# One kernel of attention and an MLP: shared q buffers with batch 3's q loaded first, block 3's sums in one round, and merged bursts of scores

## The chip, the cores and the metric

One core of a Trainium2 chip. The metric is the device time of one execution in microseconds (us). The TensorE is busy almost throughout, and an effect of 1 us is 0.2%; between executions the old kernel itself scatters by 0.8 us in the first rounds and by 1.8 to 3.3 us in later ones.

## The reference, cut to what matters

```python
# q, k, v: (8 batches, 8 heads, 1024, 64); E, F: (64, 1024)
k_proj = einsum('ks,bhsd->bhkd', E, k);  v_proj = einsum('ks,bhsd->bhkd', F, v)
attn   = softmax(q @ k_proj^T / 8)                 # 64 columns for each row
x      = (attn @ v_proj) as (8192 tokens, 512)
h      = x @ w_in                                  # 512 -> 2048
out    = (h * sigmoid(1.702 h)) @ w_out            # 2048 -> 512
```

## The kernel before

The 8192 tokens are 16 blocks of 512, two to a batch. A block runs 16 groups of four 128x512 matmuls with w_in (slots 0 to 15), then eight parts of eight with w_out (slots O to O+7, where O = 16). Attention of later blocks is put between these: `at(block, slot, ...)` says where. GpSimd (POOL) issues the loads of k, q and v, which also cast them to bf16; SyncE (SP) issues everything else in its own order: transposes of q and of the projected k, the stores of the output, and the trip of the softmax's reciprocals.

```python
def load(b):                                # on POOL's queue
    load_kv(k, kt, b, "k_sb")
    if b == 1: load_kv(v, vt, b, "v_sb")
    load_q(b)                               # eight pieces
    if b > 1:  load_kv(v, vt, b, "v_sb")    # v is last
...
def proj(b):                                # projection of k and v: 8 x (k, v)
    for j in range(J):
        for e, r in enumerate((LO, HI)):
            nc.tensor.matmul(kvps[b][r], eft(...), (kt, vt)[e][b][:, :, j, :], ...)
...
def sums(h):                                # one group: softmax sums of a whole block
    ...  nc.tensor.matmul(d_ps[e][32*p:32*p+32], ones[r, :32], expT[h][r, p, :], ...)
    ...  nc.vector.reciprocal(rden[:, e, :], d_ps[e])
def spread(h):                              # "the trip": to DRAM, back as a broadcast
    nc.sync.dma_start(out=rdr, in_=rdens.pop(h)[0:P:32])                   # 16 KB
    for e, r in enumerate((LO, HI)):                                       # 2 x 512 KB
        nc.sync.dma_start(out=rbc[h][r], in_=rdr[None, :, e, :].to_broadcast([D, HP, TB]))
def norm(h, u):                             # sums spread by the matmul itself: no trip
    eight(d_ps, [ones, ones], e);  eight(n_ps, [vqs..., ], e)
    for i in range(2):
        nc.vector.reciprocal(rd, d_ps[i])
        nc.vector.tensor_tensor(x_of(h)[:, 2*u+i, :], n_ps[i], rd, op=ALU.mult)
def values(h, u):                           # uses rbc, what the trip brings
    eight(n_ps, [vqs..., ], ...)
    ...  nc.vector.tensor_tensor(x_of(h)[...], n_ps[i], rbc[h][...], op=ALU.mult)
...
at(2, 0, proj(2), kv_out(2))
at(2, 1, norm(3, 0))
at(2, 11, norm(3, 1))
at(2, O, q_dma(3))
at(2, O + 4, scores(5, 0))
at(2, O + 6, proj(3), kv_out(3), scores(5, 1), sums(4), spread(4))
```

The softmax here doesn't subtract the row's maximum and nothing guards it: scores larger than these inputs give would overflow.

Of the kernel before, what the change touches and what calls it, by code (L numbers as in the profile page):

```python
# [9 lines left out]
F32 = mybir.dt.float32  # L10
BF16 = mybir.dt.bfloat16
# [6 lines left out]
def kernel(ctx, tc, q, k, v, E, F,  # L18
                                                     moe_w_in, moe_w_out, out):
    nc = tc.nc  # L20
    B, H, S, D = q.shape
    KP, _ = E.shape
    DM, DFF = moe_w_in.shape
    P = 128
    J = S // P
# [4 lines left out]
    TB = 512  # L30
    JB = TB // P
# [5 lines left out]
    ldpool = ctx.enter_context(tc.tile_pool(name="ldpool", bufs=1))  # L37
# [3 lines left out]
    ps_x = ctx.enter_context(tc.tile_pool(name="ps_x", bufs=4, space=PSUM))  # L41
# [8 lines left out]
    kt, vt, qt = {}, {}, {}  # L50

    def load_kv(src, dst, b, name, hs=H, js=0, jn=J):
        if b not in dst:
            dst[b] = ldpool.tile([P, H, J, D], BF16, name=name)
        sv = src[b].rearrange("h (p j) d -> p h j d", p=P)
        for h, n in [(h, hs) for h in range(0, H, hs)] if isinstance(hs, int) else hs:
            nc.gpsimd.dma_start(out=dst[b][:, h:h + n, js:js + jn], in_=sv[:, h:h + n, js:js + jn])  # L57

    def load_q(b):
        qt[b] = ldpool.tile([P, J, H, D], BF16, name="q_sb")  # L60
        qv = q[b].rearrange("h (p j) d -> p j h d", p=P)
        for j in range(J):
            nc.gpsimd.dma_start(out=qt[b][:, j], in_=qv[:, j])  # L63

    def load(b):
        load_kv(k, kt, b, "k_sb")
        if b == 1:
            load_kv(v, vt, b, "v_sb")
        load_q(b)
        if b > 1:  # L70
            load_kv(v, vt, b, "v_sb")

# [3 lines left out]
    def load_w_in(i):  # L76
        sl = slice(i * DFF // 8, (i + 1) * DFF // 8)
        nc.gpsimd.dma_start(out=w_in_sb[:, :, sl], in_=w_in_v[:, :, sl])
# [4 lines left out]
    load_kv(k, kt, 0, "k_sb", ((0, 4), (4, 2), (6, 2)))  # L83
    ident = consts.tile([P, P], BF16)
    make_identity(nc, ident)
    load_kv(q, qt, 0, "q0_sb", H, 0, 2)
    load_kv(v, vt, 0, "v_sb", ((0, 4), (4, 2), (6, 2)))
    load_kv(q, qt, 0, "q0_sb", H, 2, 2)
    for i in range(6):
        load_w_in(i)  # L90
    load_kv(q, qt, 0, "q0_sb", H, JB, JB)
    for i in range(6, 8):
        load_w_in(i)
    for i in range(4):
# [34 lines left out]
    def f_tile(shape, dt=F32):  # L129
        return ps_f.tile(shape, dt, name="f_ps")  # L130
# [23 lines left out]
    def eft(j, cols=slice(0, 2 * KP)):  # L154
        return efts[j // (J // 2)][:, j % (J // 2), cols]
# [4 lines left out]
    def proj(b):  # L160
        def go():
            kvps[b] = f_tile([P, H, D])
            for j in range(J):
                for e, r in enumerate((LO, HI)):
                    nc.tensor.matmul(kvps[b][r], eft(j, slice(e * KP, (e + 1) * KP)),  # L165
                                     (kt, vt)[e][b][:, :, j, :],
                                     start=(j == 0), stop=(j == J - 1))
        return go
# [38 lines left out]
    def v_out(b, v_ps):  # L207
        vv = v_ps[HI].rearrange("k (u x) d -> k u x d", x=4)
        for r, xs_ in ((LO, X_LO), (HI, X_HI)):
            if b == 1:  # L210
                vx = vx1[r, :, :D].rearrange("k (u x) d -> k u x d", x=4)
                nc.vector.tensor_copy(vx[:, :, xs_], vv[:, :, xs_])
            nc.vector.tensor_copy(vqs[b % 2][r].rearrange("k (u e) d -> k u e d", e=2), vv[:, :, xs_, :])

    def kv_out(b):
        def go():
            ps = kvps.pop(b)
            k_b = att.tile([KP, H, D], BF16, name="k_b")
            nc.vector.tensor_copy(k_b, ps[LO])  # L219
            if b > 1:  # L220
                nc.sync.dma_start_transpose(out=kts[b % 2], in_=k_b.rearrange("k h d -> k (h d)"))
            v_out(b, ps)
            kbs[b] = k_b
        return go
# [31 lines left out]
    def eight(outs, lhsTs, rhss):  # L256


        for i, ro in ((0, (LO, HI)), (1, (HI, LO))):
            for c in range(0, KP, 32):  # L260
                for ri, r in zip((LO, HI), ro):
                    nc.tensor.matmul(outs[i][r.start + c:r.start + c + 32], lhsTs[i][ri, c:c + 32], rhss[i][ri],  # L262
                                     start=True, stop=True)

    def scores(h, u, half=None):
        b, c = divmod(h, NB2)
        j0, n = (c * JB, JB) if half is None else (c * JB + half * JB // 2, JB // 2)
        ts = slice(j0 * P - c * TB, (j0 + n) * P - c * TB)

        def go():  # L270
            if h not in expT:
                expT[h] = att.tile([P, HP, TB], BF16, name="expT", bufs=3)
            s_ps = [f_tile([P, n * P]) for _ in range(2)]
            eight(s_ps, [kts[b % 2][:, 2 * u + i, :] for i in range(2)],
                 [q0s[half][u][:, :, i, :] if h == 0 else qT[b][:, j0:j0 + n, 2 * u + i, :]
                   for i in range(2)])
            for i in range(2):
                nc.scalar.activation(expT[h][:, 2 * u + i, ts], s_ps[i], AF.Exp, scale=scale)  # L278
        return go
# [4 lines left out]
    def x_of(h):  # L284
        if h not in xT:
            xT[h] = att.tile([P, KC, TB], BF16, name="xT", bufs=3)
        return xT[h]

    def sums(h):


        def go():
            d_ps = [ps_x.tile([P, TB], F32, name="x_ps") for _ in range(2)]
            for p in range(HP):
                for e in range(2):
                    r = HI if (p + e) % 2 else LO
                    nc.tensor.matmul(d_ps[e][32 * p:32 * p + 32], ones[r, :32], expT[h][r, p, :], start=True, stop=True)  # L297
            rden = att.tile([P, 2, TB], F32, name="rden", bufs=1)
            for e in range(2):
                nc.vector.reciprocal(rden[:, e, :], d_ps[e])  # L300
            rdens[h] = rden
        return go

    def spread(h):
        def go():
            rdr = dram.tile([HP, 2, TB], F32, name="rdr")
            nc.sync.dma_start(out=rdr, in_=rdens.pop(h)[0:P:32])
            rbc[h] = att.tile([P, HP, TB], F32, name="rbc")
            for e, r in enumerate((LO, HI)):
                nc.sync.dma_start(out=rbc[h][r], in_=rdr[None, :, e, :].to_broadcast([D, HP, TB]))  # L310
        return go

    def norm(h, u):
        def go():
            e = [expT[h][:, 2 * u + i, :] for i in range(2)]
            d_ps = [ps_x.tile([P, TB], F32, name="x_ps") for _ in range(2)]
            eight(d_ps, [ones, ones], e)
            n_ps = [ps_x.tile([P, TB], F32, name="x_ps") for _ in range(2)]
            eight(n_ps, [vqs[h // NB2 % 2][:, 2 * u + i, :] for i in range(2)], e)
            for i in range(2):  # L320
                rd = att.tile([P, TB], F32, name="rdn")
                nc.vector.reciprocal(rd, d_ps[i])  # L322
                nc.vector.tensor_tensor(x_of(h)[:, 2 * u + i, :], n_ps[i], rd, op=ALU.mult)
        return go

    def values(h, u):
        def go():
            n_ps = [ps_x.tile([P, TB], F32, name="x_ps") for _ in range(2)]
            eight(n_ps, [vqs[h // NB2 % 2][:, 2 * u + i, :] for i in range(2)],
                  [expT[h][:, 2 * u + i, :] for i in range(2)])  # L330
            for i in range(2):
                nc.vector.tensor_tensor(x_of(h)[:, 2 * u + i, :], n_ps[i], rbc[h][:, 2 * u + i, :], op=ALU.mult)  # L332
        return go
# [82 lines left out]
    def at(j, slot, *fs):  # L416
        fill.setdefault((j, slot), []).extend(fs)

    O = FC
    Q = 2 * FC  # L420
# [25 lines left out]
    q_tr0(1, 1, DV)  # L446

    order = [(half, fc) for fcs in (range(12), range(12, FC)) for half in range(2) for fc in fcs]
    at(0, 0, scores(0, 0, 1))
    at(0, 1, scores(0, 1, 1), gelu_table)  # L450
    for p in range(HP):
        at(0, 2 + p, tok(0, p, 1))
        at(0, 5 + p, x_tr(0, p, 1))
    at(0, 20, q_tr(2))
    at(0, 23, q_tr(3))
    for u in range(2):
        at(0, Q + u, scores(1, u))
    at(0, Q + 1, gelu_table)
    for p in range(HP):
        at(0, Q + (2, 4, 6, 7)[p], tok(1, p, 0), tok(1, p, 1))  # L460
# [3 lines left out]
    at(1, 13, lambda: k_tr(1, kbs[1], 0))  # L464
    at(1, 1, q_dma(1, 0, JB), q_dma(1, JB, JB))
    for u in range(2):
        at(1, O + u, scores(2, u))
        at(1, O + 3 + u, scores(3, u))
        at(2, O + 2 * u, scores(4, u))
    for p in range(HP):  # L470
        at(1, O + 2 + p, tok(2, p, 0), tok(2, p, 1))
        at(1, O + 3 + p, x_tr(2, p, 0), x_tr(2, p, 1))
    at(1, O + 5, gelu_table)
    at(1, O + 4, q_dma(2))
    at(2, 0, proj(2), kv_out(2))
    at(2, 1, norm(3, 0))
    at(2, 11, norm(3, 1))
    at(2, O, q_dma(3))
    at(2, O + 4, scores(5, 0))
    at(2, O + 6, proj(3), kv_out(3), scores(5, 1), sums(4), spread(4))  # L480
    at(2, O + 7, gelu_table)
    for b in range(4, B):
        j = NB2 * b - 4
# [65 lines left out]
```

## Time and profile before

| | |
|---|---|
| time, median of 4 | 512.28 us (511.82 to 512.57) |
| TensorE busy | 504.4 of 510.4 us |
| its listed waits after 21 us | one, of 0.2 us |
| POOL's loads, share of the DMA engines | 51.4% over the span |

TensorE sets the time. The prediction below shows the lines that say so. A line of a timeline has start, length (both in us), engine, source line, operation, output<-inputs, tile form, size and count, and in brackets the idle time before it and what ended it (PE is the TensorE, DVE VectorE, ACT ScalarE, SPq the queue of SyncE). f_ps and x_ps are tiles in PSUM, gT and xT what the large matmuls read, k_sb, q_sb and v_sb the loads, rden, rdr and rbc the reciprocals on their trip. One more view matters for what came: the stretches in us from the start, with the busy time and the number of instructions of each engine, the granted TensorE clock, the mean share of the DMA engines (more than 1 when packets overlap) and GB/s.

```profile
117.00:119.00 2.00, 2.00 (x11) 0.78 (x8) 0.00 (x0) 0.59 (x1) 0.00 (x0) 1.00 1.30 295
119.00:121.00 2.00, 2.00 (x25) 0.86 (x29) 0.00 (x0) 0.00 (x0) 0.00 (x0) 1.00 1.23 74
121.00:123.00 2.00, 2.00 (x25) 0.80 (x24) 1.83 (x4) 1.09 (x2) 1.38 (x2) 1.00 0.00 0
```

The DMA engines are loaded without a break until about 120 us and idle only at 121. The projection of batch 3, which needs v(3), the last load in the queue, begins at 119.11. v(3) was issued at 105.97 and landed 10.6 us later, so it had 2.5 us of room. (The time from issue to landing, here and below, is from the DMA view of a window about the issue.) I did not look at this before I predicted.

### The profile page before, as it was taken

What the parts mean: (1) busy time and instruction counts of PE and PEld (TensorE: products, weight loads), DVE (VectorE), ACT (ScalarE), POOL (GpSimd) and SP (SyncE); (2) the same over time, 40 slices, a digit from 0 to 9 for tenths busy, and PEclk for the clock granted to TensorE, in tenths of its full rate; (3) what the DMA queues carried; (4) which work ended last, traced back from release to release, by engine and by line L of the source; (5) the groups of instructions that cost most, each with busy time, mean ns of one, the idle gap of its engine ahead of it and who ended that gap; (6) DMA issues with size and microseconds to landing.
All of it is one profiled execution on the core that took longest, in us unless ns stands there. A gap on an engine that the chain in (4) does not pass through costs nothing.

```text
span 510.4 us, 7234 instructions
## 1 busy us (share of the span) xinstructions
PE 504.4 (99%) x3090; PEld 232.0 (45%) x3090; DVE 165.6 (32%) x221; ACT 264.3 (52%) x443; POOL 78.1 (15%) x97
## 2 busy tenths in 40 slices
PE   8999999999999999999999999999999999999997
PEld 4684444444444444444444444444444444444444
DVE  5513114765161623216161341616214161611000
ACT  2675564555637456471746637374563737244351
POOL 7442051514200051000510033000000000000000
PEclk9999999999999999999999999999999999999999
DMA  9999999999999099651998249990603205050202
GB/s 172 197 203 207 212 140 165 225 177 138 166 239 211 1 209 187 144 129 39 213 167 202 49 99 212 116 241 1 171 1 74 93 9 157 1 166 1 82 1 82
DMA packets 124752, 67.64 MB, mean 133 GB/s; under 512 B 92288, under 2 KB 116096, under 8 KB 122800
## 3 DMA queue, kind: packets, MB, share of 16 engines
q0 software_dynamic: 84400, 29.37, 51.4%
q1 hardware_dynamic: 40240, 37.56, 29.3%
q8 instruction: 24, 0.39, 0.3%
q10 hardware_dynamic: 80, 0.26, 0.2%
q14 instruction: 8, 0.07, 0.0%
HBM read 71.83 MB, written 16.97 MB: 174 GB/s over the span
## 4 chain that ended last, share of the span: by engine, by line
PE 94%; DMA 4%; POOL 1%; issue 0%; DVE 0%; ACT 0%; POOLq 0%
PE f_ps L405 43%; PE f_ps L373 43%; PE f_ps L165 3%; DMA w_in_sb<-in_moe_w_in_dram 2%; PE f_ps L262 2%; DMA v_sb<-in_v_dram 2%; PE x_ps L262 1%; PE x_ps L297 1%; POOL k_sb L57 0%; PE x_ps L359 0%; PE x_ps L344 0%; PE f_ps L397 0%; PE f_ps L244 0%; POOL q_sb L57 0%; POOL v_sb L57 0%
## 5 line engine op out<-in xcount | busy, mean ns | idle before, releaser
L405 PE MATMUL f_ps<-w_out_sb,gT 128*128 128x512 bf16 x1008 | 227.2, 379 | 0.0
L373 PE MATMUL f_ps<-xT,w_in_sb 128*128 128x512 bf16 (+1 forms) x1088 | 226.4, 367 | 0.3 <-DMA w_in_sb<-in_moe_w_in_dram 0.2
L376 ACT ACTIVATE gT<-f_ps 128x512 bf16<-128x512 f32 (+1 forms) x270 | 151.8, 574 | 61.4 <-PE f_ps L373 60.2
L373 PEld LDWEIGHTS <-w_in_sb 128*128 128x128 bf16 x1088 | 105.3, 98 | 116.2 <-issue 1.7
L405 PEld LDWEIGHTS <-gT 128*128 128x128 bf16 x1008 | 95.6, 98 | 120.5 <-issue 11.3
L408 ACT COPY o_sb<-f_ps 128x512 f32<-128x512 f32 x63 | 37.0, 587 | 126.8 <-PE f_ps L405 117.0
L332 DVE TENSOR_TENSOR xT<-x_ps,rbc 128x512 bf16<-128x512 f32 x48 | 30.9, 686 | 201.3 <-PE x_ps L262 124.9
L300 DVE RECIPROCAL rden<-x_ps 128x512 f32<-128x512 f32 x24 | 78.7, 3322 | 10.3 <-PE x_ps L297 10.3
L63 POOL DMA_DIRECT2D q_sb<-in_q_dram x56 | 49.1, 901 | 52.0 <-DMA k_sb<-in_k_dram 39.2
L278 ACT ACTIVATE expT<-f_ps 128x512 bf16<-128x512 f32 (+1 forms) x68 | 35.1, 571 | 32.7 <-PE f_ps L262 32.6
L57 POOL DMA_DIRECT2D k_sb<-in_k_dram x10 | 8.4, 846 | 175.5 <-PE f_ps L165 159.1
L219 DVE CAST k_b<-f_ps 64x512 bf16<-64x512 f32 x7 | 4.8, 683 | 46.8 <-PE f_ps L165 46.8
L278 ACT ACT_TABLE_LOAD x13 | 16.7, 1283 | 4.7 <-PE f_ps L262 4.5
L282 ACT ACT_TABLE_LOAD x14 | 18.0, 1283 | 0.2
L322 DVE RECIPROCAL rdn<-x_ps 128x512 f32<-128x512 f32 x4 | 13.4, 3353 | 0.8 <-PE x_ps L262 0.8
L165 PE MATMUL f_ps<-k_sb,eft 128*64 128x512 bf16 x56 | 13.4, 382 | 0.0
L165 PE MATMUL f_ps<-v_sb,eft 128*64 128x512 bf16 x56 | 13.4, 381 | 0.0
L399 DVE COPY o_sb<-f_ps 128x256 f32<-128x256 f32 x1 | 0.4, 424 | 38.6 <-issue 38.6
L135 PE MATMUL x_ps<-zeros 128*128 128x512 bf16 x34 | 11.2, 450 | 1.2 <-DVE zeros L106 1.2
L262 PE MATMUL f_ps<-qT,kt 64*32 64x512 bf16 x240 | 12.3, 386 | 0.0
L262 PE MATMUL x_ps<-expT,vq 64*32 64x512 bf16 x208 | 10.2, 377 | 0.0
L262 PEld LDWEIGHTS <-kt 64*32 64x32 bf16 x272 | 3.9, 88 | 13.7 <-issue 13.5
(71 smaller groups left out, 128.4 us busy)
## 6 DMA issues: line engine op xcount, KB each, us to landing
out_dram<-o_sb SPq DMA_DIRECT2D x15, 1024.0 KB
rbc<-rdr SPq DMA_DIRECT2D x24, 512.0 KB
k_sb<-in_k_dram POOLq DMA_DIRECT2D x7, 1024.0 KB, 13.3
v_sb<-in_v_dram POOLq DMA_DIRECT2D x7, 1024.0 KB, 10.6
q_sb<-in_q_dram POOLq DMA_DIRECT2D x56, 128.0 KB, 12.0
w_in_sb<-in_moe_w_in_dram POOLq DMA_DIRECT2D x8, 256.0 KB, 12.2
w_out_sb<-in_moe_w_out_dram POOLq DMA_DIRECT2D x4, 512.0 KB, 14.7
out_dram<-o_sb SPq DMA_DIRECT2D x3, 256.0 KB
```

The lines of the kernel that those rows point to most:

```text
L63: nc.gpsimd.dma_start(out=qt[b][:, j], in_=qv[:, j])
L165: nc.tensor.matmul(kvps[b][r], eft(j, slice(e * KP, (e + 1) * KP)), (kt, vt)[e][b][:, :, j, :], start=(j == 0), stop=(j == J - 1))
L262: nc.tensor.matmul(outs[i][r.start + c:r.start + c + 32], lhsTs[i][ri, c:c + 32], rhss[i][ri], start=True, stop=True)
L278: nc.scalar.activation(expT[h][:, 2 * u + i, ts], s_ps[i], AF.Exp, scale=scale)
L282: nc.scalar.preload_act_table(AF.Gelu_apprx_sigmoid)
L300: nc.vector.reciprocal(rden[:, e, :], d_ps[e])
L322: nc.vector.reciprocal(rd, d_ps[i])
L332: nc.vector.tensor_tensor(x_of(h)[:, 2 * u + i, :], n_ps[i], rbc[h][:, 2 * u + i, :], op=ALU.mult)
L373: nc.tensor.matmul(h_ps, w_in_sb[:, kc, fc * P:(fc + 1) * P], xT[j][:, kc, ts], start=(kc == 0), stop=(kc == KC - 1))
L376: nc.scalar.activation(gts[j][:, fc, ts], h_ps, AF.Gelu_apprx_sigmoid)
L405: nc.tensor.matmul(o_ps[n], gts[j][:, fc, n * P:(n + 1) * P], w_out_sb[:, fc, :], start=(fc == 0), stop=(fc == FC - 1))
L408: nc.scalar.copy(osb[j][:, n, :], o_ps.pop(n))
```

## The change

Intent: fewer switches between the large matmuls and the small 64x32 tiles, one group of small matmuls fewer, and a load order that clears the way for the new trip of block 3. Its core (cut and condensed):

```diff
+    def q_buf(order):                      # two q buffers for all batches
+        return ldpool.tile([P, J * H * D], BF16, name="q_sb", bufs=2).rearrange(...)
     def load(b):
+        if b == 3:
+            load_q(b)
         load_kv(k, kt, b, "k_sb")
...
-        load_q(b)
+        if b != 3:
+            load_q(b)
...
-            s_ps = [f_tile([P, n * P]) for _ in range(2)]
+            s_ps = [(x_tile() if x else f_tile([P, TB]))[:, :n * P] for _ in range(2)]
...
-    at(0, 0, scores(0, 0, 1))
-    at(0, 1, scores(0, 1, 1), gelu_table)
+    at(0, 1, scores(0, 0, 1), scores(0, 1, 1, True), gelu_table)
-        at(0, Q + u, scores(1, u))
+        at(0, Q, scores(1, u, None, u > 0))
-        at(1, O + u, scores(2, u))
-        at(1, O + 3 + u, scores(3, u))     # now both at O + 6
-        at(2, O + 2 * u, scores(4, u))
+        at(1, O, scores(2, u, None, u > 0))
+        at(2, O, scores(4, u, None, u > 0))
+        at(2, O + 3 * u, values(3, u))
...
-    at(2, 0, proj(2), kv_out(2))
-    at(2, 1, norm(3, 0))
-    at(2, 11, norm(3, 1))
+    at(2, 0, proj(2), kv_out(2), sums(3), spread(3))
-    at(2, O + 4, scores(5, 0))
+    at(2, O + 3, scores(5, 0))
```

More of the change, by code (lines that the diff above doesn't have):

```diff
@@ L57, in load_kv @@
             nc.gpsimd.dma_start(out=dst[b][:, h:h + n, js:js + jn], in_=sv[:, h:h + n, js:js + jn])
+    def q_buf(order):
+        return ldpool.tile([P, J * H * D], BF16, name="q_sb", bufs=2).rearrange(
+            f"p ({order} d) -> p {order} d", d=D, h=H)
     def load_q(b):
-        qt[b] = ldpool.tile([P, J, H, D], BF16, name="q_sb")
+        qt[b] = q_buf("j h")
         qv = q[b].rearrange("h (p j) d -> p j h d", p=P)
@@ L85 @@
     make_identity(nc, ident)
-    load_kv(q, qt, 0, "q0_sb", H, 0, 2)
+    qt[0] = q_buf("h j")
+    load_kv(q, qt, 0, "", H, 0, 2)
     load_kv(v, vt, 0, "v_sb", ((0, 4), (4, 2), (6, 2)))
-    load_kv(q, qt, 0, "q0_sb", H, 2, 2)
+    load_kv(q, qt, 0, "", H, 2, 2)
     for i in range(6):
         load_w_in(i)
-    load_kv(q, qt, 0, "q0_sb", H, JB, JB)
+    load_kv(q, qt, 0, "", H, JB, JB)
     for i in range(6, 8):
@@ L263, in eight, with x_tile, scores @@
                                      start=True, stop=True)
-    def scores(h, u, half=None):
+    def x_tile():
+        return ps_x.tile([P, TB], F32, name="x_ps")
+    def scores(h, u, half=None, x=False):
         b, c = divmod(h, NB2)
@@ L472 @@
         at(1, O + 3 + p, x_tr(2, p, 0), x_tr(2, p, 1))
-    at(1, O + 5, gelu_table)
+    for u in range(2):
+        at(1, O + 6, scores(3, u, None, u > 0))
+    at(1, O + 6, gelu_table)
     at(1, O + 4, q_dma(2))
-    at(2, 0, proj(2), kv_out(2))
-    at(2, 1, norm(3, 0))
-    at(2, 11, norm(3, 1))
+    at(2, 0, proj(2), kv_out(2), sums(3), spread(3))
     at(2, O, q_dma(3))
-    at(2, O + 4, scores(5, 0))
+    at(2, O + 3, scores(5, 0))
     at(2, O + 6, proj(3), kv_out(3), scores(5, 1), sums(4), spread(4))
```

## The prediction

> **What bounds the kernel now.** I read the engine shares first, then the chain of work that ended last, then the waits of the TensorE, then the timelines of blocks 0 to 3. A "block" is 512 tokens: 64 matmuls with w_in, then 64 with w_out. The attention of later blocks is put between them.
>
> ```profile
> PE 504.4 (99%) x3090; PEld 232.0 (45%) x3090; DVE 165.6 (32%) x221; ACT 264.3 (52%) x443; POOL 78.1 (15%) x97
> ...
> PE 94%; DMA 4%; POOL 1%; issue 0%; DVE 0%; ACT 0%; POOLq 0%
> ...
> PE f_ps L373 <- DMA w_in_sb<-in_moe_w_in_dram: 0.2, 1, 0.2
> ...
> 27.51 4.98 PE L373 MATMUL f_ps<-xT,w_in_sb 128*128 128x256 bf16 x44 [0.20 <-DMA w_in_sb<-in_moe_w_in_dram]
> ```
>
> TensorE is the bound and hardly waits: after 21 us the only listed wait is 0.2 us for a piece of w_in, at 27.51. So DVE or POOL time is worth nothing in itself, and the change gains only what it takes off the TensorE's own row. What a small burst costs there stands in the PE timeline of block 2 and of its neighbours:
>
> ```profile
> 105.59 1.89 PE L405 MATMUL f_ps<-w_out_sb,gT 128*128 128x512 bf16 x8
> 107.41 0.41 PE L262 MATMUL f_ps<-qT,kt 64*32 64x512 bf16 x8
> 107.75 3.63 PE L405 MATMUL f_ps<-w_out_sb,gT 128*128 128x512 bf16 x16
> ...
> 137.07 1.89 PE L405 MATMUL f_ps<-w_out_sb,gT 128*128 128x512 bf16 x8
> 138.89 0.41 PE L262 MATMUL f_ps<-qT,kt 64*32 64x512 bf16 x8
> 139.11 0.40 PE L297 MATMUL x_ps<-expT,ones 64*32 64x512 bf16 x8
> 139.33 0.40 PE L262 MATMUL x_ps<-expT,vq 64*32 64x512 bf16 x8
> 139.66 10.53 PE L405 MATMUL f_ps<-w_out_sb,gT 128*128 128x512 bf16 x48
> ```
>
> Read the start column. A stream of 128x512 matmuls goes at 0.216 us each (16 from 107.75 to 111.31, less the switch). Eight take 1.73, so of the 2.16 us from 105.59 to 107.75 the burst takes 0.43. The burst of three groups at 138.89 takes 139.66-137.07-1.73 = 0.86. Hence a group of eight 64*32 matmuls costs 0.215 us and the two changes of tile form round a burst cost 0.215 us together, however many groups it holds. These two numbers size the gain.
>
> **What the Trainium skill says.** "TensorEngine Tiling (Array Packing)", section Key Properties: changing the tiling mode drains the TensorE. The trace agrees: 0.215 us per burst. "DMA: Bandwidth & Descriptors", section Queues, rings and completion order: each DMA engine goes round the queues packet by packet, so a transfer on one queue is slowed by what another queue has pending; the trace agrees (the reciprocals' trip through DRAM, below). "ScalarE: Activation LUTs", section What ACT_TABLE_LOAD costs: about 1283 ns; the trace has 1283 ns for each of 27 loads. The change keeps their number, so I give that no time.
>
> **The change, part by part.**
>
> *Scores in one burst.* Merged are the two half-width bursts of block 0's second half, and the pairs for blocks 1, 2, 3 and 4: five bursts fewer. The first lies before 27.51, where the TensorE waits for w_in whose transfer the change does not touch: its 0.2 to 0.35 us become a longer wait, worth 0. Blocks 1, 2, 3: 3 x 0.215 = 0.65 us, all ahead of the projection of batch 2. Block 4's: 0.215.
>
> *Block 3's sums in one round.* Each old norm was one burst of two groups, at slots 1 and 11 of block 2. That makes four groups; the new form has one group of sums and two of values: one group less, 0.215. Bursts in block 2 before: slots 1, 11, O, O+2, O+4 (and O+6, kept), where O is the first slot of the w_out half. After: the sums directly behind the projection, O with three groups (scores and values), O+3 with two. Behind a projection a group costs less than alone: the projection with two groups takes 121.52-119.11 = 2.41 us against 1.85 for one alone (64.56 to 66.41), so two groups cost 0.56, and of that 0.43 is the groups. From five separate bursts to two and a cheap one: 2.4 x 0.215 = 0.51, block 4's merge included. Block 2 in all: 0.51 + 0.215 = 0.73 us.
>
> *DVE.* It loses four reciprocals of 3.353 us and adds two of 3.322, minus 6.8 us, off the path. Added are three small DMAs and 1 MB of broadcast for block 3.
>
> *Two q buffers, q(3) first.* The old POOL waits for a free q buffer sum to 1.1 us (on the qT transposes, at 93.62), so a second buffer alone buys nothing. Its worth is the order: load(3) can send q(3) right behind v(2), near 80 us, while k(3) must wait for the projection of batch 2 (before: issued at 91.64). The DMA queue then has k(3) and v(3) left for 91 to 113 us in place of k, q and v.
>
> Upper sum: 0.65 + 0.73 = 1.38 us, to 510.9.
>
> **The rivals.**
>
> *1. v(2) takes the gain ahead of batch 2's projection.*
>
> ```profile
> 89.42 0.40 PE L165 MATMUL f_ps<-k_sb,eft 128*64 128x512 bf16 x1
> 89.49 0.38 PE L165 MATMUL f_ps<-v_sb,eft 128*64 128x512 bf16 x1
> ...
> 360.04 0.40 PE L165 MATMUL f_ps<-k_sb,eft 128*64 128x512 bf16 x1
> 360.05 0.40 PE L165 MATMUL f_ps<-v_sb,eft 128*64 128x512 bf16 x1
> ```
>
> In a later batch the v matmul starts 0.01 us behind the k matmul; for batch 2 it is 0.07. v(2) was issued at 78.82, and v lands in about 10.6 us: 89.4. So I read that v(2) lands just when it is needed. Its chain runs from the end of projection 1 (k(2) issued at 66.78) through DMA, and only the 0.215 us of block 1's merge comes ahead of it. Then about 0.43 of the 0.65 us turns into a wait, and q(3) pending behind v(2) may delay it a little more (0 to 1.5 us). I take 0.5 lost.
>
> *2. The reciprocals come too late for values(3,1).* The new sums go to DRAM and back as a broadcast. Two such trips in the old trace, in the SyncE and DVE timelines:
>
> ```profile
> 129.31 0.62 SPq L307 DMA_DIRECT2D rdr<-rden  x1
> 134.75 1.35 SPq L310 DMA_DIRECT2D rbc<-rdr  x2
> ...
> 147.70 1.29 DVE L332 TENSOR_TENSOR xT<-x_ps,rbc 128x512 bf16<-128x512 f32 x2 [1.55 <-DMA rbc<-rdr]
> ...
> 357.26 0.54 SPq L307 DMA_DIRECT2D rdr<-rden  x1
> 359.13 1.25 SPq L310 DMA_DIRECT2D rbc<-rdr  x2
> ```
>
> With loads of q, k and v in flight the trip took 147.70-129.31 = 18.4 us; late in the kernel 366.88-357.26 = 9.6. On the old clock the reciprocals of block 3 run from 93.0 (behind the casts of batch 2) to 99.6, so rbc lands between 109.2 and 118.0. The TensorE gets to O+3 after projection end 91.31 + sums 0.33 + 15 groups of w_in 12.96 + one part of w_out 1.73 + the burst 0.86 + three parts 5.18 = 112.4. values(3,1) needs the two PSUM tiles of values(3,0): four x_ps tiles, taken in turn by sums, values, scores, values. They are free only after the two multiplications that use rbc, 1.29 us after it lands. So rbc has to land by 111.1. The best trip leaves 1.9 us of slack; the congested one stalls the TensorE 6.9 us. With q(3) already gone, k(3) and v(3) are still in flight from 99.6 to about 113, and q_dma(3) is issued behind rbc. From the volumes I would expect 12 to 15 us for the trip, a stall of 0.5 to 3.5 us. Against it: q(3) first and O+3 look chosen to make the trip short, so I give 45% to no stall. Weighted: 0.9 us lost.
>
> *3. ScalarE holds PSUM back.* At block 1's O+6 four exponentials (4 x 0.54), a table load (1.28) and the copy of the last output tile come in a row, so that copy ends about 4.5 us after the burst begins, and the projection of batch 2 wants an f_ps tile after 3.2. If tiles went strictly in turn it would stall 1.3 us. But at 123.25 block 3's first matmul started before the copy (123.45) of the tile that would have been its turn, so tiles are handed out in the order of release, and the projection gets one of the score tiles. I give this 10%.
>
> **Range and chances.** 512.24 - 1.38 + 0.5 (rival 1) + 0.9 (rival 2), less the rounding of a guess, is 512.2; the median of the cases lies a little lower, since the stall has a long tail: I predict 512.0. With neither rival: 510.9, and runs scatter 0.4, so the low end is 510.6. With 2.5 to 3.5 us of stall: 514.8. Ten microseconds either way would need a stall or a gain larger than anything found: within 2%, 97.5 in 100.
>
> **What would show it.** Steps right: scores bursts of 16 matmuls at about 0.65 us each way; block 2 with one L297 group behind the projection; DVE busy down by about 7 us; q_sb issues near 80 us. Rival 1: the v matmul of batch 2 clearly behind the k matmul, or a wait of TensorE on v_sb. Rival 2: a gap in the TensorE's row before the L262 values group at O+3 (about 112 us), and block 3's trip over 11.5 us. Rival 3: a gap before the projection at about 89 us with L408 as its releaser. The prediction is wrong if the gap at O+3 is over 4 us, or if v(2) is late by more than 2 us because q(3) shares its DMA engines; or, the other way, if the wait for w_in at 27.51 also moves earlier.

## The result, and the profile after

517.26 us, the median of 4 (516.41 to 519.74), beside 512.28. The ratio is 1.0106 with a 95% interval of 1.007 to 1.0142. Ratios here and below are the mean time of one kernel's fast runs over that of the other's of the same rounds, so not quite the ratio of the medians. The change is slower by some 5 us (1%), and outside the range that I gave. No kernel differs from the old one by 2%; what is told apart below is told by the intervals.

The traced execution is the fastest of the four (516.41, span 514.6 in place of 510.4). Its TensorE waits, from the view of who waited for whom (engine, tile and line; releaser; us in total, times, longest):

```profile
PE f_ps L173 <- DMA v_sb<-in_v_dram: 4.4, 2, 3.0
```

L173 is the projection's line. Two waits, both for a v. In the TensorE's timeline, projection 2, then projection 3:

```profile
88.98 0.40 PE L173 MATMUL f_ps<-k_sb,eft 128*64 128x512 bf16 x1
90.84 0.38 PE L173 MATMUL f_ps<-v_sb,eft 128*64 128x512 bf16 x1 [1.46 <-DMA v_sb<-in_v_dram]
...
119.68 0.40 PE L173 MATMUL f_ps<-k_sb,eft 128*64 128x512 bf16 x1
123.04 0.38 PE L173 MATMUL f_ps<-v_sb,eft 128*64 128x512 bf16 x1 [2.95 <-DMA v_sb<-in_v_dram]
```

The same place in the old kernel, with the first matmul of block 3:

```profile
119.11 0.40 PE L165 MATMUL f_ps<-k_sb,eft 128*64 128x512 bf16 x1
119.11 0.40 PE L165 MATMUL f_ps<-v_sb,eft 128*64 128x512 bf16 x1
...
123.25 1.03 PE L373 MATMUL f_ps<-xT,w_in_sb 128*128 128x512 bf16 x4
```

The brackets give the idle time; counted from start to start the second gap is 3.36 us, where it was 0.00 before. With these numbers the whole loss up to block 3 can be added up. Old, k and v of projection 2: 89.42 and 89.49. New: block 3's first matmul at 127.15. So v of projection 2 comes 1.35 us later; from there to projection 3 it takes 28.84 in place of 29.62, a gain of 0.78; then 3.36 of new gap; then 4.11 in place of 4.14. Together 1.35 - 0.78 + 3.36 - 0.03 = 3.90, which is 127.15 - 123.25. The rest of the kernel adds another 0.3.

The gain is there. The two old bursts at slots 1 and 11 have become one group at 92.66, directly behind the projection; in the TensorE's timeline O is one burst of three groups, and the second values follow at O+3:

```profile
107.78 0.41 PE L270 MATMUL f_ps<-qT,kt 64*32 64x512 bf16 x8
108.01 0.40 PE L270 MATMUL x_ps<-expT,vq 64*32 64x512 bf16 x8
108.23 0.40 PE L270 MATMUL x_ps<-qT,kt 64*32 64x512 bf16 x8
...
113.84 0.41 PE L270 MATMUL x_ps<-expT,vq 64*32 64x512 bf16 x8
```

SyncE's timeline of the same stretch shows the DMA side, and VectorE's shows when the trip's result came:

```profile
84.39 11.02 SPq L260 DMA_TRANSPOSE qT<-q_sb  x1
95.46 0.60 SPq L423 DMA_DIRECT2D out_dram<-o_sb  x1
96.11 1.22 SPq L229 DMA_TRANSPOSE kt<-k_b  x1
100.98 0.63 SPq L318 DMA_DIRECT2D rdr<-rden  x1
107.43 1.32 SPq L321 DMA_DIRECT2D rbc<-rdr  x2
109.11 15.02 SPq L260 DMA_TRANSPOSE qT<-q_sb  x1
...
118.45 2.48 DVE L343 TENSOR_TENSOR xT<-x_ps,rbc 128x512 bf16<-128x512 f32 x4 [17.49 <-DMA rbc<-rdr]
```

The trip took 118.45 - 100.98 = 17.5 us. Before, the two transposes of q at 84 and 111 us took 6.85 and 6.72 us; now they take 11.02 and 15.02. The small transposes of the projected k (1.22 us; 2.14 before) are not longer. The plainest number is that of v(3): it was issued at 96.23, nearly 10 us earlier than in the old kernel, and took 26.8 us to land in place of 10.6. (The listed TensorE busy time, 497.9 us, is not comparable with the old: 3031 matmuls are recorded beside 3082 weight loads, so some 50 records are missing.)

### The profile page after: what moved, and what is told of

It reads as the page before. It is cut to its first block, busy times and chain, and to the rows that moved or that the text cites. A ratio compares the mean times of both kernels' runs of the same rounds, so it can differ in the third digit from the quotient of the medians.

```text
span 514.6 us, 7152 instructions
## 1 busy us (share of the span) xinstructions
PE 497.9 (97%) x3031; PEld 232.2 (45%) x3082; DVE 158.2 (31%) x219; ACT 264.0 (51%) x443; POOL 78.2 (15%) x97
## 4 chain that ended last, share of the span: by engine, by line
PE 85%; DMA 11%; issue 2%; ACT 1%; DVE 0%; POOL 0%; POOLq 0%
PE f_ps L384 40%; PE f_ps L416 37%; DMA v_sb<-in_v_dram 7%; DMA k_sb<-in_k_dram 3%; PE f_ps L173 3%; PE f_ps L270 2%; PE x_ps L270 1%; PE f_ps L181 1%; PE x_ps L143 1%; PE x_ps L308 1%; PE x_ps L370 0%; PE f_ps L408 0%; ACT L293 0%; PE f_ps L241 0%; PE x_ps L355 0%
## 5 line engine op out<-in xcount | busy, mean ns | idle before, releaser
L416 PE MATMUL f_ps<-w_out_sb,gT 128*128 128x512 bf16 x975 | 220.8, 379 | 4.0 <-issue 3.5
L416 PEld LDWEIGHTS <-gT 128*128 128x128 bf16 x1008 | 95.9, 98 | 121.6 <-issue 11.8
L343 DVE TENSOR_TENSOR xT<-x_ps,rbc 128x512 bf16<-128x512 f32 x52 | 33.4, 686 | 218.8 <-PE x_ps L270 124.6
L311 DVE RECIPROCAL rden<-x_ps 128x512 f32<-128x512 f32 x26 | 85.3, 3322 | 10.4 <-PE x_ps L308 10.3
L289 ACT ACTIVATE expT<-f_ps 128x512 bf16<-128x512 f32 (+1 forms) x58 | 30.1, 573 | 33.2 <-PE f_ps L270 33.2
L173 PE MATMUL f_ps<-v_sb,eft 128*64 128x512 bf16 x56 | 13.3, 381 | 4.4 <-DMA v_sb<-in_v_dram 4.4
L173 PE MATMUL f_ps<-k_sb,eft 128*64 128x512 bf16 x56 | 13.8, 383 | 0.0
L173 PEld LDWEIGHTS <-eft 128*64 128x64 bf16 x112 | 6.2, 109 | 12.0 <-issue 8.0
L270 PE MATMUL f_ps<-qT,kt 64*32 64x512 bf16 x208 | 10.7, 386 | 0.0
L362 DVE TENSOR_TENSOR x_sb<-x_ps,rd 128x256 bf16<-128x256 f32 x22 | 9.3, 425 | 0.8
## 6 DMA issues: line engine op xcount, KB each, us to landing
v_sb<-in_v_dram POOLq DMA_DIRECT2D x7, 1024.0 KB, 11.8
```

The lines of the kernel that those rows point to most:

```text
L173: nc.tensor.matmul(kvps[b][r], eft(j, slice(e * KP, (e + 1) * KP)), (kt, vt)[e][b][:, :, j, :], start=(j == 0), stop=(j == J - 1))
L270: nc.tensor.matmul(outs[i][r.start + c:r.start + c + 32], lhsTs[i][ri, c:c + 32], rhss[i][ri], start=True, stop=True)
L289: nc.scalar.activation(expT[h][:, 2 * u + i, ts], s_ps[i], AF.Exp, scale=scale)
L343: nc.vector.tensor_tensor(x_of(h)[:, 2 * u + i, :], n_ps[i], rbc[h][:, 2 * u + i, :], op=ALU.mult)
L416: nc.tensor.matmul(o_ps[n], gts[j][:, fc, n * P:(n + 1) * P], w_out_sb[:, fc, :], start=(fc == 0), stop=(fc == FC - 1))
```

## The experiments

Two theories after the first look. **Theory 1**: the new load order is the cause. q(3) in front shares the DMA engines with v(2), stretches the transposes, and pushes the store of block 1 into the time of k(3) and v(3). **Theory 2**: the trip of block 3 is the cause. Its 1 MB of broadcast comes in a stretch in which the DMA engines have nothing to spare, and v(3), last in the queue, lands late. Every kernel below gave correct results. All were timed in five rounds; the old kernel's medians were 512.98, 512.73 and 512.80 in the three series.

### First series: one part each

**The changed kernel with the old load order** (k, q, v for batch 3).

```diff
-        if b == 3: load_q(b)
         load_kv(k, kt, b, "k_sb")
...
-        if b != 3: load_q(b)
+        load_q(b)
```

> The changed kernel with batch 3's loads in the old order k, q, v (two q buffers kept). Theory 1 (q(3) in front shares the DMA engines with v(2), stretches the qT(2) transposes and pushes the store of block 1 into the window of k(3) and v(3)): the wait for v at projection 2 falls from 1.46 us to under 0.7, v(3) is then issued later, near 106 us, and the wait at projection 3 is under 1; time 511 to 513. Theory 2 (the new 1 MB broadcast of block 3's reciprocals delays v(3)): the wait at projection 2 also goes, but the one at projection 3 stays at 2 us or more; time 514 to 517.

518.09 us, ratio 1.0099 (1.0082 to 1.0116). The wait at projection 2 fell from 1.46 to 0.42 us; the one at projection 3 rose to 3.48. Theory 1 asked for 511 to 513 and falls as the main cause. The time is a little above what theory 2 gave.

**The old kernel with only the two q buffers and q(3) first.**

```diff
+        if b == 3: load_q(b)      # and q_buf as in the change
         load_kv(k, kt, b, "k_sb")
```

> The old kernel with only the two shared q buffers and q(3) first. Theory 1: v(2) lands about 1.4 us late and there is a wait at projection 2; the qT(2) transposes take about 11 us in place of 6.9; v(3) late too; 514 to 516. Theory 2: only the 1 to 1.5 us at projection 2; 513 to 514.

513.61 us, ratio 1.0014 (0.9995 to 1.0033). The trace, of the slowest of its six executions (515.16), has a wait of 1.81 us for v at projection 2 and none at projection 3. So the load order does delay v(2), as expected of both, but no loss is resolved in the times. v(3) landed 23.7 us after its issue at 97.82, only 0.6 us before projection 3: in time, but with less room than the 2.5 us of the old kernel.

**The old kernel with only the merged bursts.**

```diff
+    at(0, 1, scores(0, 0, 1), scores(0, 1, 1, True), gelu_table)
+        at(0, Q, scores(1, u, None, u > 0))
+        at(1, O, scores(2, u, None, u > 0))      # scores(3) both at (1, O + 6)
+        at(2, O, scores(4, u, None, u > 0))      # norm(3, .) as before
```

> The old kernel with only the merged score bursts of blocks 0 to 4. Both theories: 0.43 us saved ahead of projection 2 is mostly taken by a wait for v(2), 0.2 us in block 2 stays; 511.6 to 512.2 beside 512.3.

511.99 us, ratio 0.9984 (0.9968 to 1.0): 0.8 us less, somewhat more than expected, with an interval that reaches up to no gain. At projection 2 it waits 0.29 us for v. I had expected a small loss there, but this one proves little: a kernel below without merges (no broadcast) waits 0.33 us at the same place.

**The old kernel with only block 3's sums in one round**, which brings the trip.

```diff
-    at(2, 0, proj(2), kv_out(2))
-    at(2, 1, norm(3, 0))
-    at(2, 11, norm(3, 1))
+    at(2, 0, proj(2), kv_out(2), sums(3), spread(3))
+    for u in range(2):
+        at(2, O + 3 * u, values(3, u))
```

> The old kernel with only block 3's sums in one round (and its trip through DRAM), old load order, one q buffer. Theory 1: no new wait for v at projection 2; v(3) at most 1 us late; 511.5 to 513. Theory 2: a wait of 2 us or more for v(3) at projection 3; 514 to 516.

517.76 us, ratio 1.0095 (1.0071 to 1.012): this part alone brings nearly the whole loss. One wait at projection 3, and something else behind it. The TensorE's timeline, then the stretches of 2 us:

```profile
118.92 0.40 PE L165 MATMUL f_ps<-k_sb,eft 128*64 128x512 bf16 x1
122.26 0.38 PE L165 MATMUL f_ps<-v_sb,eft 128*64 128x512 bf16 x1 [2.94 <-DMA v_sb<-in_v_dram]
```

```profile
120.00:122.00 2.00, 0.00 (x0) 0.00 (x0) 0.00 (x0) 0.00 (x0) 0.00 (x0) 1.00 1.29 118
122.00:124.00 2.00, 1.74 (x14) 1.08 (x14) 0.00 (x0) 0.00 (x0) 0.00 (x0) 0.81 1.25 282
124.00:126.00 2.00, 2.00 (x22) 0.32 (x19) 1.01 (x2) 0.49 (x1) 0.86 (x1) 0.50 0.77 174
126.00:128.00 2.00, 2.00 (x9) 0.78 (x8) 1.96 (x3) 0.60 (x2) 1.49 (x3) 0.84 0.63 42
```

The third column from the right is the granted clock. After the idle time it goes down to 0.50 and is back at full only near 127. From the v matmul at 122.26 to block 3's first matmul at 127.95 it takes 5.69 us; in the old kernel the same stretch takes 4.14. So the wait costs 3.3 us and then 1.55 us more. (The changed kernel with the old load order, which waits 3.48 us, drops its clock too and takes the same 5.69 us.) The Trainium skill has this in "TensorE: Matmul & The Clock Gate", section Why this matters for your kernels: "No PE-idle gaps >~3µs between matmul bursts". This trace agrees roughly: 2.94 us were enough. The traced run of the changed kernel had 2.95 us and kept its clock, so a wait of this length is at the edge. Its three untraced siblings have a mean clock of 0.996 in place of 0.999 and are 0.6 to 3.3 us slower; that they had such a drop is likely, but only their means show it.

### Second series: the trip by itself, fewer bytes, another order

**The old kernel with a trip that nothing reads.** norm stays; the reciprocals of its first half also go to DRAM and come back as 1 MB of broadcast.

```diff
+            if u == 0:
+                rdr = dram.tile([HP, 2, TB], F32, name="rdr")
+                for i in range(2):
+                    nc.sync.dma_start(out=rdr[:, i, :], in_=rds[i][0:P:32])
+                dummy = att.tile([P, HP, TB], F32, name="rbc")
+                for e, r in enumerate((LO, HI)):
+                    nc.sync.dma_start(out=dummy[r], in_=rdr[None, :, e, :].to_broadcast([D, HP, TB]))
```

> The old kernel (norm for block 3, old load order) with one more trip through DRAM in block 2 that nothing reads: the reciprocals of block 3's first half are written to DRAM and read back as a 1 MB broadcast, near 101 to 117 us. Theory 2 (the broadcast's traffic is what delays v(3)): a wait of 2 to 4 us for v at projection 3, a TensorE clock that then drops to 0.5 for some us in most executions, 515 to 518. Rival (the sums themselves, the earlier arrival of the TensorE at projection 3 by 0.2 us or the placement of values is the cause): no wait, 512.3 to 513.3.

516.00 us, ratio 1.0063 (1.0039 to 1.0086). Its trace is of the slowest of its executions (518.34):

```profile
120.49 0.40 PE L165 MATMUL f_ps<-k_sb,eft 128*64 128x512 bf16 x1
123.56 0.59 PE L165 MATMUL f_ps<-v_sb,eft 128*64 128x512 bf16 x1 [2.66 <-DMA v_sb<-in_v_dram]
```

The clock went to 0.50 behind it. The compute of this kernel is the old one's, and nobody waits for the trip. v(3) took 15.6 us to land in place of 10.6. So the trip alone delays v(3): theory 2 holds.

**The changed kernel with the trip in bf16**, half the bytes.

```diff
-            rden = att.tile([P, 2, TB], F32, name="rden", bufs=1)
+            rden = att.tile([P, 2, TB], BF16, name="rden3", bufs=1)   # h == 3; rdr, rbc too
```

> The changed kernel with block 3's reciprocals and their broadcast in bf16: half the bytes. Theory 2: the wait at projection 3 falls from about 3 us by half or more, below the length at which the clock drops; the wait of about 1.5 us at projection 2 stays; 513 to 515. Rival (the count of transfers or the trip's latency matters, not its bytes): as the changed kernel, 516 to 519.

521.49 us, ratio 1.0146 (1.0112 to 1.0181): neither expectation's number. The listed waits, and the reason:

```profile
PE x_ps L270 <- DVE xT L347: 5.1, 1, 5.1
PE f_ps L173 <- DMA v_sb<-in_v_dram: 2.1, 1, 2.1
```

The wait of 2.1 us is that of projection 2. The 5.1 us are at values(3,1), which now wait for a PSUM tile of values(3,0) until the trip is back (VectorE's multiplications start at 119.35). This is the stall of rival 2 of the prediction. The changed kernel was spared it: there values(3,1) ran at 113.84, ahead of the first multiplication at 118.45, so it had other tiles. In the half-size kernel such tiles were free too, for the exponentials that read them were done by 112.7, and it waited all the same. So tiles were not handed out by what was free in the run; that it was settled when the program was built is my reading and not shown. The clock dropped to 0.50 in this stall too. The wait for v(3) was covered by the stall, but its landing is 26.0 us after the issue, against 26.8 with the full trip and 23.7 without a trip in the same queue order (the kernel with q(3) first only). Half the bytes took away 0.8 of some 3 us. The trip itself took 119.35 - 102.05 = 17.3 us, against 17.5. One trace each, but they speak for this experiment's rival: bytes alone are not the measure.

**The changed kernel with v before q** for batches 2 and 3.

```diff
-        if b == 3: load_q(b)
         load_kv(k, kt, b, "k_sb")
-        if b == 1:
+        if b in (1, 2, 3):
             load_kv(v, vt, b, "v_sb")
-        if b != 3: load_q(b)
+        load_q(b)
```

> The changed kernel with load order k, v, q for batches 2 and 3: 1 MB less ahead of each v in the queue. Theory 2 with this remedy: no wait for v at projections 2 and 3, no clock drop, although the broadcast of block 3 stays; the whole gain of about 1.2 us shows: 510.6 to 511.8 beside 512.3 to 513. If the broadcast delayed more than v (rbc past the need of block 3, q(3) too late for scores), new waits appear and it is above 512.

519.57 us, ratio 1.0129 (1.0109 to 1.0148). Both waits for v are gone, as meant. New ones took their place:

```profile
PE f_ps L267 <- DMA kt<-k_b: 6.6, 2, 5.1
```

q now lands last. SyncE issues in order, and the transpose of q(3) (124.97 to 137.18) stands ahead of the small transpose of the projected k (137.24), which scores(6) need near 139.6. The missing DMA time had moved to another user. I had named late q as the way in which it could fail, but not this queue.

**The merges alone with v before q for batch 2.**

> The old kernel with the merged score bursts only and load order k, v, q for batch 2. Against the run with the merges alone: its wait of 0.3 us for v at projection 2 goes, and 0.4 us less time; 511.3 to 512.0.

513.24 us, ratio 1.0004 (0.9981 to 1.0028): a miss. Projection 2 no longer waits, but with one q buffer q(3) could not start before the later transpose of q(2) was done (issued at 103.41 in place of 93.69), and v(3) then cost 0.60 us at projection 3. Nothing was won.

### Third series: the dose, the clock, and a try at a better kernel

**The trip that nothing reads, with one broadcast of two** (0.5 MB), and **with none**.

```diff
-                for e, r in enumerate((LO, HI)):
-                    nc.sync.dma_start(out=dummy[r], in_=rdr[None, :, e, :].to_broadcast([D, HP, TB]))
+                nc.sync.dma_start(out=dummy[LO], in_=rdr[None, :, 0, :].to_broadcast([D, HP, TB]))
```

> The old kernel with the idle trip of block 3 as before, but only one of its two broadcasts: 0.5 MB in place of 1. Theory 2 (the volume of the broadcast on full DMA engines delays v(3)): v(3) lands about 2.5 us earlier than with 1 MB, so the wait at projection 3 is 0 to 1 us and the clock does not drop; 512.5 to 514. Rival (what counts is that the SyncE queue is held by the trip, not its volume): the wait stays above 2 us, 515 to 517.

> The old kernel with only the small writes of the idle trip (2 x 8 KB to DRAM) and no broadcast. Theory 2: as the old kernel, no wait at projection 3, 512.3 to 513. Rival (the small writes on SyncE's queue): a wait remains.

513.34 us, ratio 1.0012 (0.9997 to 1.0027), and 512.99 us, ratio 1.0006 (0.9993 to 1.0018). Projection 3 with half a broadcast, then with none:

```profile
119.69 0.40 PE L165 MATMUL f_ps<-k_sb,eft 128*64 128x512 bf16 x1
119.84 0.38 PE L165 MATMUL f_ps<-v_sb,eft 128*64 128x512 bf16 x1
```

```profile
119.57 0.40 PE L165 MATMUL f_ps<-k_sb,eft 128*64 128x512 bf16 x1
119.57 0.40 PE L165 MATMUL f_ps<-v_sb,eft 128*64 128x512 bf16 x1
```

From k to v it is 0.00 us without a broadcast, 0.15 with 0.5 MB, 3.07 with 1 MB. v(3) took 10.5, 13.2 and 15.6 us from issue to landing: each of the two broadcasts adds about 2.5 us, the first uses up the slack, and the second is all loss. The small writes on SyncE's queue cost nothing here. This series halves the bytes and the number of transfers together, so it does not say which of the two counts; the half-size trip above, with the same number of transfers, speaks against the bytes alone.

**The sums alone with 13 idle matmuls ahead of projection 3**, to keep the TensorE awake.

```diff
-    at(2, O + 6, proj(3), ...
+    at(2, O + 6, lambda: warm(13), proj(3), ...
```

> The run with the sums alone, with 13 idle matmuls of 128x512 (2.8 us) put ahead of projection 3, in the place of its wait for v(3). If a part of its loss is the TensorE clock that drops to 0.5 after the wait: v(3) lands when it did (about 122), the clock stays at 1.0 and 1.2 to 1.6 us come back, 516 to 516.6 beside 517.8. If the drop has nothing to do with the idle TensorE: 517.5 to 518.5 and the clock drops all the same.

516.97 us, ratio 1.0083 (1.007 to 1.0096). The clock stays at 1.0: from the v matmul at 123.62 to block 3 at 127.73 it is 4.11 us, in place of 5.69. v itself landed later, above all since it was issued 0.9 us later in this trace (1.06 us were still waited for behind the 2.8 us of idle work), so 0.8 us of the median came back, less than expected, and the intervals of the two ratios overlap. The mean clock is 0.999 or 1.0 in all five executions, where the sums alone had 0.993 to 0.997 in four of six. So the drop is due to the idle TensorE; the times do not resolve its size.

**Merges, two q buffers, v before q for batch 2 only, and the first norm behind the projection.**

> The merged score bursts without the new sums, two shared q buffers in the order k, v, q for batch 2 and k, q, v for batch 3, and the first norm of block 3 directly behind the projection of batch 2. No wait for v at projections 2 and 3; 0.3 to 0.4 us below the merges alone, so 511.3 to 511.9 if the old kernel is at 512.7. If q(2) last in its load pushes the store of block 1 and with it v(3): a wait at projection 3 of up to 1 us and no gain over the merges alone.

513.33 us, ratio 1.0017 (0.9998 to 1.0036): a miss. q(2) last stretched SyncE's list again: 1.26 us of wait for the transposed k at O, 0.55 us for v(3). The best version remains the merges alone, 0.9984 (0.9968 to 1.0): clearly below the changed kernel, and not clearly below the old one.

## Why the prediction was wrong, point by point

1. **Bursts and groups: right.** I gave 0.65 us ahead of projection 2. Its k matmul came at 88.98 in place of 89.42, though block 0's first w_out group came 0.25 later (38.72 and 38.47): 0.69. I gave 0.73 for block 2; it was 0.78. That the merge ahead of 27.51 is worth nothing can't be read from this trace, whose start ran late (0.64 us at 19.5); in the trace of the merges alone the wait for w_in was still there (0.16 us), and nothing had been gained by the first w_out group (38.60).

2. **Rival 1, v(2): mechanism right, size wrong.** The term "I take 0.5 lost" measured 1.79 us in the trace: from k to v 1.86 us in place of 0.07. v(2) landed 11.8 us after its issue, and 10.6 in the old kernel and in the changed one with the old order. So q(3) behind it cost 1.2 us, inside my 0 to 1.5; I had set nearly nothing of that span into the 0.5.

3. **Rival 2, the trip: wrong twice.** I took 12 to 15 us and it was 17.5. And the stall at O+3 did not come, since "four x_ps tiles, taken in turn" was not how they were handed out. I had used the order of release against rival 3 and not here. The half-size trip shows that the stall can come (5.1 us), so neither rule foretells it. That it did not come here was luck: my 45% for it rested on a short trip, and the trip was long.

4. **The step that failed** is the sentence "Added are three small DMAs and 1 MB of broadcast for block 3", which stood under VectorE's savings as off the path, and its companion, that the DMA queue "then has k(3) and v(3) left for 91 to 113 us in place of k, q and v". I asked when the new traffic would arrive and never what it would push back. I charged it nothing; the gap at projection 3 is 3.36 us, and the unread trip of the same size (3.07 us, and none without its broadcast) shows that the broadcast is its cause and not a coincidence. Nor did q(3) first empty the queue: with the old order the waits were 0.42 us at projection 2 and 3.48 at projection 3, with the new one 1.46 and 2.95. v(3) did go out 10 us earlier, but landed no earlier.

5. **Not in the prediction at all**: a wait of about 3 us may also lower the TensorE's clock to half for some 3 us, 1.55 us more. One such drop would explain about half of the way from 516.41 to the slowest execution, 519.74; neither that nor the rest was traced.

6. **Rival 3** did not occur: the trace has no wait ahead of projection 2 with the output copy as its releaser.

What stays open: why half the bytes hardly shortened the trip or the delay of v(3), and so what it is in the broadcast that costs (the count of transfers or packets was not varied alone); how many of the untraced executions had the clock drop; and the effect of the load order beside the sums, where 1.0106 and 1.0099 cannot be told apart.

## What to carry to other kernels

A transfer that nobody needs soon still has a price when the DMA engines are full: ask which transfer is last in the queue, how much slack it has, and charge a new transfer to that one. A reordering of loads in such a stretch mostly chooses who waits, above all where one engine issues its transfers in order. And in this kernel a TensorE wait of about 3 us or more had to be charged up to 1.55 us more than its length, since the clock was lowered with it in five of the six traces that have such a wait.

## What the Trainium skill lacked or had wrong

- "TensorE: Matmul & The Clock Gate", section Why this matters for your kernels: the section's limit of about 3 us is a little high, and not sharp. Listed waits of 2.66, 2.94, 3.48 and twice 5.1 us lowered the clock to 0.50; one of 2.95 did not. The drop cost 1.55 us in two traces.
- "DMA: Bandwidth & Descriptors", section Queues, rings and completion order: it says that queues share an engine packet by packet, which agrees, but no size follows from it. Here the same transposes of q issued by SyncE took 6.7 to 6.9 us in the old kernel and 11.0 and 15.0 in the changed one, and v(3) on the other queue landed 10.5, 13.2 and 15.6 us after its issue beside no, half and a whole broadcast.
- No page that I read says how long a small result's trip through DRAM and back as a broadcast takes under load: 9.6 us late in the old kernel, 17.3 to 18.9 us with loads in flight, and 17.3 in place of 17.5 with half the bytes.
